# Head of the last product: rebuilding the weight bits with ScalarE's help, and another order of the splits

## The chip, the cores and the metric

The kernel runs on one core of a Trainium2 chip. TensorE (PE in the profile) does the matrix products, VectorE (DVE), ScalarE (ACT) and GpSimd (POOL) prepare operands and drain results, and SyncE (SP) issues the transfers. The metric is device microseconds of one execution; lower is better. Before the change three runs took 577.69, 578.14 and 578.86 us; the median is 578.14 us.

## The reference

Causal attention over 2 batches, 12 heads, 448 positions and 64 dimensions gives `x` of 896 x 768. Two dense blocks follow:

```python
h = x @ w_in                    # 768 -> 2048
g = h * np.cos(h)
y = g @ w_out                   # 2048 -> 768
a = y @ w_a                     # 768 -> 1536
b = y @ w_b
out = (a * b @ w_out2).astype(np.float32)   # 1536 -> 768
```

The weights arrive as 64-bit floats; the kernel gets each as two 32-bit words, low and high.

## The kernel before, in words

All activations are held transposed, features on the 128 partitions, tokens in two halves of 448 columns (b = 0, 1). A product of 32-bit precision is made of three passes on TensorE: each operand is split into a rounded part `hi` and a rest `lo`, and hi·hi, hi·lo and lo·hi are summed in PSUM.

**The weights.** SyncE loads one chunk of 64-bit words into a tile `w_raw` (three buffers, L84), and the chunk is then rebuilt as 32-bit floats in place. `w_scale` (L97, ScalarE) multiplies the high words, read as floats, by 2^-112, which moves the exponent. `w_shift` (L105, VectorE) shifts the low words right by 29, which leaves their top three bits. `w_pack` (L110, VectorE) shifts the scaled high words left by 3 and puts the three bits in; `w_sign` (L118, VectorE) puts the sign in. Then `w_hi` (L143, ScalarE) rounds the chunk and `w_lo` (L154, POOL) subtracts; the end of `w_lo` frees the buffer, and the load of the chunk three places later is issued (L160).

**The last product** is a seven-multiplication scheme over 2 x 2 blocks. A chunk of its weight `w_o2` is a "quad" of four 128 x 128 blocks (512 columns); there are 18, three passes p of six quads q. For a quad the scaled high words go into a PSUM bank named `high` (tag `z`, one buffer, L102), so the next quad's scaling waits until `w_sign` has read it. `w_sums` (L125, VectorE) adds three instructions that form the sums of blocks, in the place of the high words. The other operand is a*b, for six pairs of feature tiles c0 to c5: VectorE multiplies (L674) and forms sums t1, t2, t4 (`sums`, L624); `halves` (L633) splits the seven operands b11, t2, b12, t1, b21, b22, t4 into hi (ScalarE) and lo (VectorE or POOL, as a list names them). c0 to c3 are done well before; c4 and c5 only at the end of the a and b products.

**The order** is the program's own: each engine works through its instructions in the order in which the code issues them, and waits where an operand is missing. `both` (L666) does one pair of a and b products and hangs preparation work `between` and `after` them. `bits_to(i)` rebuilds quads up to i, `halves_of(i)` also splits quad i, and `scale_next` issues the scaling of the next quad not yet rebuilt. In the first pass (L781) step q splits quad q+3, prepares some operands of c5 (`some`), rebuilds quad q+4 and multiplies quad q by seven operands (21 matmuls). Quads 4 and 5 are then multiplied operand by operand, and each finished result is taken out of PSUM by VectorE (`take`, L726).

Of the kernel before, what the change touches and what calls it, by code (L numbers as in the profile page):

```python
# [11 lines left out]
I32 = mybir.dt.int32  # L12
ACTF = mybir.ActivationFunctionType
ALU = mybir.AluOpType
# [2 lines left out]
P = 128  # L17
TWO_PI = 6.283185307179586
SIGN = -0x80000000


def f32(ap):
    return ap.bitcast(F32)
# [3 lines left out]
def tile_causal_attention_cos_gate_bilinear(  # L27
# [16 lines left out]
    nc = tc.nc  # L44
# [5 lines left out]
    N_IN, N_Y, N_C = w_in.shape[0], w_out.shape[0], w_a.shape[0]  # L50
# [15 lines left out]
    QUAD = 4 * P  # L66
# [4 lines left out]
    queue = []  # L71
# [8 lines left out]
    raw, scaled, chunks = {}, {}, {}  # L80
# [13 lines left out]
    def is_quad(i):  # L94
        return queue[i][0] in QUADS

    def w_scale(i):  # L97


        if i < len(queue):  # L100
            high = f32(raw[i][:, :, 1])
            scaled[i] = bank("z", "high")[:, :QUAD] if is_quad(i) else high  # L102
            nc.scalar.activation(scaled[i], high, ACTF.Copy, scale=2.0**-112)  # L103

    def w_shift(i):  # L105
        if i < len(queue):
            low = raw[i][:, :, 0]
            nc.vector.tensor_single_scalar(low, low, 29, op=ALU.logical_shift_right)  # L108

    def w_pack(i):  # L110

        if i < len(queue):
            low, high = raw[i][:, :, 0], scaled[i].bitcast(I32)
            nc.vector.scalar_tensor_tensor(  # L114
                out=low, in0=high, scalar=3, in1=low, op0=ALU.logical_shift_left, op1=ALU.bitwise_or
            )

    def w_sign(i):  # L118
        if i < len(queue):
            low, high = raw[i][:, :, 0], scaled.pop(i).bitcast(I32)  # L120
            nc.vector.scalar_tensor_tensor(  # L121
                out=low, in0=high, scalar=SIGN, in1=low, op0=ALU.bitwise_and, op1=ALU.bitwise_or
            )

    def w_sums(i):  # L125


        if i < len(queue) and is_quad(i):
            t = f32(raw[i]).rearrange("p (s n) w -> p s w n", s=4)
            nc.vector.tensor_tensor(out=t[:, 0, 1], in0=t[:, 0, 0], in1=t[:, 1, 0], op=ALU.subtract)  # L130
            a22 = t[:, 2, 0].unsqueeze(1).to_broadcast([P, 2, P])
            nc.vector.tensor_tensor(out=t[:, 1:3, 1], in0=t[:, 0], in1=a22, op=ALU.add)
            nc.vector.tensor_tensor(out=t[:, 3, 1], in0=t[:, 3, 0], in1=t[:, 2, 1], op=ALU.subtract)
# [40 lines left out]

    def w_bits(i):

        w_shift(i)
        w_pack(i)
        w_sign(i)
        w_sums(i)  # L180

    def w_halves(i):

# [13 lines left out]
    def bank(tag, name):  # L197
        return psum.tile([P, 512], F32, tag=tag, name=name, bufs=BUFS[tag])

    def product(kind, f, acts, name, release, parts=1, pump=True):  # L200

        ps = bank(next(cycle), name)[:, :S]
        n = len(acts)
        t = j = 0
        while t < n:
            hi, lo, k = chunks[kind, f, j]
            terms = [(hi, c, part) for c in range(k) for part in range(2)] + [(lo, c, 0) for c in range(k)]
            for i, (w, c, part) in enumerate(terms):
                nc.tensor.matmul(  # L209
                    ps,  # L210
                    w[:, c * P : (c + 1) * P],
                    acts[t + c][part],
                    start=t == 0 and i == 0,
                    stop=t + k == n and i == len(terms) - 1,
                )
                if (i + 1) % (len(terms) // parts) == 0 and i + 1 < len(terms):
                    yield ps
            t += k
            if release:
                del chunks[kind, f, j]  # L220
            if kind != "in" and pump:
                w_pump()
            j += 1
        yield ps
# [92 lines left out]
    with ExitStack() as actx:  # L317
# [11 lines left out]
        for o in (0, S):  # L329
            for e in range(2):  # L330
                half = mask[e * D : (e + 1) * D, o : o + D]
                nc.gpsimd.affine_select(
                    out=half,
# [174 lines left out]
        def at(fn, i):  # L508
# [25 lines left out]
            (14, w_load, 1),  # L534
            (18, w_load, 2),
            (20, w_scale, 0),
            (22, w_shift, 0),
            (24, w_pack, 0),
# [27 lines left out]
    with tc.manual_schedule():  # L566
# [46 lines left out]
        def plain_tile(q, name):  # L613
            if (q, name) not in plain_tiles:
                pool, tag = plain[q][name]
                plain_tiles[q, name] = pool.tile([P, S], F32, tag=tag, name=f"c{q}_{name}")
            return plain_tiles[q, name]
# [30 lines left out]
        o2_first = len(queue) - (N_Y // 2) * N_Q  # L648
        bits = [o2_first]

        def scale_next():
            if bits[0] not in scaled:
                w_scale(bits[0])

        def bits_to(i):
            while bits[0] <= i:
                scale_next()
                w_bits(bits[0])
                bits[0] += 1

        def halves_of(i):
            bits_to(i)
            scale_next()
            w_halves(i)

        def both(f, b, between=None, after=None, pump=True):  # L666

            q, k = divmod(f, 2)
            ps_b = next(product("b", f, y[b], "b", b == B - 1, pump=pump))
            bs = work.tile([P, S], F32, tag="r", name="bs", bufs=3)  # L670
            nc.scalar.activation(bs, ps_b, ACTF.Copy)  # L671
            between()
            ps_a = next(product("a", f, y[b], "a", b == B - 1, pump=pump))
            nc.vector.tensor_tensor(out=plain_tile(q, f"b{k + 1}{b + 1}"), in0=ps_a, in1=bs, op=ALU.mult)  # L674
            after()

        def items(n):
            def go():
                for _ in range(n):
                    next(todo, None)  # L680
            return go
# [7 lines left out]
        def mixed(*steps):  # L689
            def go():  # L690
                for fn, i in steps:
                    if fn:
                        fn(o2_first + i)
                    else:
                        items(i)()
            return go
# [2 lines left out]
        both(N_C - 2, 0, lambda: None, mixed((bits_to, 0)), False)  # L699
        both(N_C - 1, 0, mixed((bits_to, 1)), lambda: None, False)  # L700
        todo = itertools.chain(sums(IN_G), halves(IN_G, RAWS))
        both(N_C - 2, 1, mixed((None, 4), (halves_of, 0), (None, 1)), mixed((halves_of, 1), (None, 3)), False)
        free[IN_G + 1].insert(0, spare.pop())
        last_sums = sums(IN_G + 1)
        next(last_sums)
        both(N_C - 1, 1, mixed((halves_of, 2), (None, 3)), lambda: None, False)
        assert next(todo, None) is None
        free[IN_G + 1] += free[IN_G]

# [38 lines left out]
                add(kept["v"], ps, kept["v"])  # L748
                store(p, 1, 0, kept["v"])

        BY_DVE = ("b11", "t2", "t1", "b22")
        for _ in last_sums:
            pass
        late = halves(IN_G + 1, BY_DVE)

        DOUBLE = N_Q - 2

        def some(k):
            for _ in range(k):
                next(late)  # L760

        def multiply(p, q, names):
            hi, lo, _ = chunks["o2", p, q]
            for name in names:
                if q == 0:
                    banks[name] = bank(next(cycle), f"o_{name}")[:, :S]
                x_hi, x_lo = cq[q][name, "hi"], cq[q][name, "lo"]
                w = slice(OPS[name] * P, (OPS[name] + 1) * P)
                for i, (w_part, x_part) in enumerate(((hi, x_hi), (hi, x_lo), (lo, x_hi))):
                    nc.tensor.matmul(  # L770
                        banks[name],
                        w_part[:, w],
                        x_part,
                        start=q == 0 and i == 0,
                        stop=q == N_Q - 1 and i == 2,
                    )

        for p in range(N_Y // 2):
            banks, kept = {}, {}
            i = o2_first + p * N_Q  # L780
            for q in range(DOUBLE):  # L781
                halves_of(i + q + 3)
                if p == 0:
                    some((0, 4, 3, 0)[q])
                if (p, q) not in ((0, 3), (1, 0), (1, 1)):
                    bits_to(i + q + 4)
                multiply(p, q, OPS)
                del chunks["o2", p, q]
            for step, name in enumerate(OPS):
                for q in range(DOUBLE, N_Q):  # L790
                    multiply(p, q, [name])
                take(p, name, banks[name], kept)
                if step == (5 if p == 0 else 0):
                    halves_of(i + DOUBLE + 3)
                if step == 6 and p:
                    bits_to(i + N_Q + 2)
            for q in range(DOUBLE, N_Q):
                del chunks["o2", p, q]
            halves_of(i + N_Q + 2)
            if p:  # L800
                bits_to(i + N_Q + 3)
# [56 lines left out]
```

## Time and profile before

| What | Value |
|---|---|
| Runs, median (lowest to highest) | 578.14 us (577.69 to 578.86) |
| The profiled execution | 578.23 us, of which the span of instructions is 576.4 us |
| TensorE busy | 565.1 us, 98% of the span |
| VectorE / ScalarE / POOL busy | 400.0 / 286.2 / 267.4 us |
| Mean granted clock of TensorE | 0.993 of full speed |

The profiled execution is 0.09 us above the median of the runs and holds 1.83 us outside its span. Matmuls overlap, so TensorE's progress is read from the starts of its matmuls: about 0.20 us apart at full clock for 448 columns. A bracket at the end of a row names the idle time of the engine just before it and what ended it.

### The profile page before, as it was taken

Reading aid. Unit: us, or ns where it says so; the run is one execution under the profiler, and the core shown is the slowest. Engines: PE = TensorE matmul, PEld = TensorE weight load, DVE = VectorE, ACT = ScalarE, POOL = GpSimd, SP = SyncE. Lnnn points to the kernel's source line nnn. Section 1 sums busy time; section 2 is a strip of 40 time slices with the busy share of each in tenths; the row PEclk is TensorE's granted clock in tenths of the full one; section 3 lists DMA queues with packets and bytes.
Section 4 is the critical chain, followed back from the end, with each engine's and each line's share of the span. In section 5 each row is a group of like instructions: output and inputs, shape, how many; then the busy total and the mean of one; then the engine's idle time right before and its main releaser. Section 6 shows DMA issues by size and latency. Waiting matters only on the chain.

```text
span 576.4 us, 8792 instructions
## 1 busy us (share of the span) xinstructions
PE 565.1 (98%) x3240; PEld 502.1 (87%) x3240; DVE 400.0 (69%) x704; ACT 286.2 (50%) x582; POOL 267.4 (46%) x242
## 2 busy tenths in 40 slices
PE   8999999999999999999999999999999999989997
PEld 5666789999999999999999999999999998868796
DVE  5899937777777865464455665767676667879994
ACT  6888837777777732232224334343443415334431
POOL 4557744666666642232223223434343407454651
PEclk9999999999999999999999999999999999979999
DMA  8745211333332343433243333333333212324441
GB/s 316 265 161 215 89 56 56 109 111 110 110 109 93 109 147 98 140 101 112 82 164 110 114 109 107 109 111 109 111 109 110 73 38 77 97 65 155 145 140 64
DMA packets 16316, 67.81 MB, mean 118 GB/s; under 512 B 1808, under 2 KB 3472, under 8 KB 16272
## 3 DMA queue, kind: packets, MB, share of 16 engines
q1 hardware_dynamic: 16272, 67.25, 35.1%
q8 instruction: 25, 0.41, 0.3%
q14 instruction: 19, 0.16, 0.1%
HBM read 64.49 MB, written 2.75 MB: 117 GB/s over the span
## 4 chain that ended last, share of the span: by engine, by line
PE 82%; DVE 7%; ACT 4%; issue 3%; POOL 2%; DMA 2%; DVEq 0%; POOLq 0%; ACTq 0%
PE h L209 20%; PE y L209 20%; PE b L209 15%; PE a L209 14%; PE o_b L770 3%; PE o_t L770 3%; PE xa L484 2%; PE pt L457 2%; PE s L382 2%; DMA w_raw<-in_w_o 2%; ACT p L429 1%; POOL p L444 1%; POOL w_lo L158 1%; DVE p L405 1%; ACT w_hi L151 1%
## 5 line engine op out<-in xcount | busy, mean ns | idle before, releaser
L158 POOL TENSOR_TENSOR w_lo<-w_raw,w_hi 128x768 fp32r<-128x768 f32 (+2 forms) x94 | 149.3, 1596 | 227.4 <-ACT w_hi L151 165.3
L151 ACT ACTIVATE w_hi<-w_raw 128x768 fp32r<-128x768 f32 (+1 forms) x91 | 70.0, 778 | 172.8 <-DVE w_raw L121 119.0
L114 DVE SCALAR_TENSOR_TENSOR w_raw<-w_raw 128x768 int32<-128x768 int32 (+1 forms) x58 | 90.8, 1565 | 30.2 <-ACT w_raw L103 29.0
L121 DVE SCALAR_TENSOR_TENSOR w_raw<-w_raw 128x768 int32<-128x768 int32 (+1 forms) x58 | 56.2, 969 | 0.4
L444 POOL TENSOR_SCALAR p<-p,sums 128x448 f32<-128x448 f32 (+6 forms) x84 | 40.7, 505 | 27.5 <-DVE mn L405 26.2
L103 ACT ACTIVATE w_raw<-w_raw 128x768 f32<-128x768 f32 (+1 forms) x58 | 50.8, 876 | 0.0
L108 DVE TENSOR_SCALAR w_raw<-w_raw 128x768 int32<-128x768 int32 (+1 forms) x76 | 50.1, 659 | 0.4 <-DMA w_raw<-in_w_o 0.4
L429 ACT ACTIVATE p<-p,mn 128x448 f32<-128x448 f32 (+6 forms) x84 | 41.8, 501 | 8.4 <-DVE mn L405 8.4
L249 DVE SCALAR_TENSOR_TENSOR r<-r,h 128x448 f32<-128x448 int32 x32 | 19.7, 616 | 25.8 <-ACT r L248 25.7
L405 DVE CUSTOM_DVE_ANT_0 p<-s,mask 128x448 f32<-128x448 f32 (+6 forms) x84 | 31.9, 414 | 4.4 <-PE s L382 4.3
L103 ACT ACTIVATE high<-w_raw 128x512 f32<-128x512 f32 x18 | 11.6, 644 | 41.8 <-DVE w_raw L121 30.9
L382 PE MATMUL s<-qk_raw 64*64 64x448 f32 (+6 forms) x336 | 27.3, 399 | 0.8 <-DMA qk_raw<-in_qk 0.7
L674 DVE TENSOR_TENSOR c_b<-a,bs 128x448 f32<-128x448 f32 x24 | 14.9, 622 | 17.8 <-PE a L209 17.8
L382 PEld LDWEIGHTS s<-qk_raw 64*64 64x64 f32 x336 | 15.5, 135 | 11.5 <-issue 4.0
L248 ACT ACTIVATE r<-h 128x448 int32<-128x448 f32 x32 | 17.1, 539 | 16.0 <-PE h L209 8.3
L457 PE MATMUL pt<-ident,p 128*128 128x128 f32 x168 | 23.9, 280 | 1.0 <-POOL p L444 0.6
L484 PEld LDWEIGHTS xa<-pp,v 128*64 128x64 f32 x336 | 16.1, 137 | 9.4 <-issue 7.1
L484 PE MATMUL xa<-pp,v 128*64 128x64 f32 (+3 forms) x336 | 23.8, 293 | 0.0
L457 PEld LDWEIGHTS pt<-ident,p 128*128 128x128 f32 x168 | 18.2, 140 | 3.7 <-POOL p L444 2.0
L671 ACT ACTIVATE bs<-b 128x448 f32<-128x448 f32 x24 | 12.9, 536 | 15.9 <-PE b L209 15.9
L265 DVE SCALAR_TENSOR_TENSOR r<-r,h 128x448 f32<-128x448 f32 x32 | 19.5, 609 | 1.3 <-ACT r L260 1.3
L470 DVE COPY pp<-pt 128x512 f32<-128x512 f32 (+1 forms) x24 | 14.8, 615 | 6.4 <-PE pt L457 6.3
(357 smaller groups left out, 1671.8 us busy)
## 6 DMA issues: line engine op xcount, KB each, us to landing
w_raw<-in_w_in SPq DMA_DIRECT2D x16, 768.0 KB, 4.4
w_raw<-in_w_out SPq DMA_DIRECT2D x12, 768.0 KB, 4.4
w_raw<-in_w_b SPq DMA_DIRECT2D x12, 768.0 KB, 4.3
w_raw<-in_w_a SPq DMA_DIRECT2D x12, 768.0 KB, 4.4
w_raw<-in_w_o SPq DMA_DIRECT2D x18, 512.0 KB, 3.8
v<-in_v SPq DMA_DIRECT2D x12, 448.0 KB, 5.9
qk_raw<-in_qk SPq DMA_DIRECT2D x11, 448.0 KB, 6.5
w_raw<-in_w_out SPq DMA_DIRECT2D x6, 512.0 KB, 3.9
```

The lines of the kernel that those rows point to most:

```text
L103: nc.scalar.activation(scaled[i], high, ACTF.Copy, scale=2.0**-112)
L108: nc.vector.tensor_single_scalar(low, low, 29, op=ALU.logical_shift_right)
L114: nc.vector.scalar_tensor_tensor(out=low, in0=high, scalar=3, in1=low, op0=ALU.logical_shift_left, op1=ALU.bitwise_or)
L121: nc.vector.scalar_tensor_tensor(out=low, in0=high, scalar=SIGN, in1=low, op0=ALU.bitwise_and, op1=ALU.bitwise_or)
L151: nc.scalar.activation(pair[0][:, a:z], src, ACTF.Copy)
L158: engine.tensor_tensor(out=lo[:, a:z], in0=src, in1=f32(hi)[:, a:z], op=ALU.subtract)
L209: nc.tensor.matmul(ps, w[:, c * P : (c + 1) * P], acts[t + c][part], start=t == 0 and i == 0, stop=t + k == n and i == len(terms) - 1,)
L382: nc.tensor.matmul(T["s", i + c][q, o : o + WIDTH[j]], t[h, Q_COL[j] : Q_COL[j] + D], t[h, FIRST[j] : FIRST[j] + WIDTH[j]], start=True, st ...
L429: nc.scalar.activation(t, t, ACTF.Exp, bias=T["mn", n][:, c], scale=-1.0, accum_out=row_sum(n, j))
L444: nc.gpsimd.tensor_scalar(out=t, in0=t, scalar1=row_sum(n, j), scalar2=1.0, op0=ALU.mult, op1=ALU.mult)
L457: nc.tensor.transpose(dst, p_bufs[n % N_P][:, o : o + P], ident)
L484: nc.tensor.matmul(ps[e * D : (e + 1) * D, o * D : w * D], t[:, k, e], p[:, :, :, q].rearrange("p s l q -> p (s l) q") if k < 3 else p[:, ...
```

## The change

It touches only the 18 quads of `w_o2` and the order of the work around the start of the last product.

```diff
+TOP_SCALE = 2.0**-29 * (1 - 2.0**-10)
+TOP_BIAS = 7.5 * 2.0**-10 - 0.5
...
             high = f32(raw[i][:, :, 1])
-            scaled[i] = bank("z", "high")[:, :QUAD] if is_quad(i) else high
-            nc.scalar.activation(scaled[i], high, ACTF.Copy, scale=2.0**-112)
+            nc.scalar.activation(high, high, ACTF.Copy, scale=2.0**-112)
+            scaled[i] = high
+            if is_quad(i):
+                scaled[i] = bank("z", "top")[:, :QUAD].bitcast(I32)
+                low = raw[i][:, :, 0].bitcast(mybir.dt.uint32)
+                nc.scalar.activation(scaled[i], low, ACTF.Copy, bias=TOP_BIAS, scale=TOP_SCALE)
...
     def w_bits(i):
-        w_shift(i)
-        w_pack(i)
-        w_sign(i)
-        w_sums(i)
+        if i < len(queue):
+            low, high, top = raw[i][:, :, 0], raw[i][:, :, 1], scaled.pop(i)
+            for out_, by, op in ((top, SIGN, ALU.bitwise_and), (low, 3, ALU.logical_shift_left)):
+                nc.vector.scalar_tensor_tensor(out=out_, in0=high, scalar=by, in1=top, op0=op, op1=ALU.bitwise_or)
+            w_sums(i)
...
         def scale_next():
-            if bits[0] not in scaled:
+            if bits[0] in raw and bits[0] not in scaled:
                 w_scale(bits[0])
...
-        both(N_C - 2, 1, mixed((None, 4), (halves_of, 0), (None, 1)), mixed((halves_of, 1), (None, 3)), False)
+        items(4)()
+        bits_to(o2_first + 2)
+        items(2)()
+        both(N_C - 2, 1, mixed((None, 1), (halves_of, 0), (None, 4)), mixed((w_halves, 1)), False)
...
-        both(N_C - 1, 1, mixed((halves_of, 2), (None, 3)), lambda: None, False)
+        both(N_C - 1, 1, mixed((w_halves, 2), (bits_to, 3)), lambda: None, False)
...
-        BY_DVE = ("b11", "t2", "t1", "b22")
+        BY_DVE = ("b12", "b21", "b22")
...
                 halves_of(i + q + 3)
-                if p == 0:
-                    some((0, 4, 3, 0)[q])
                 if (p, q) not in ((0, 3), (1, 0), (1, 1)):
                     bits_to(i + q + 4)
+                if p == 0:
+                    some((5, 2, 0, 0)[q])
                 multiply(p, q, OPS)
```

ScalarE now scales the high words in place in SBUF and, in a second instruction, turns the low words (as unsigned integers) into their top three bits, in the PSUM bank. VectorE puts the sign into that bank and then makes the packed word, two instructions in place of three. Quad 2 and quad 3 are rebuilt earlier, and for c5 another set of lo parts is VectorE's: three (b12, b21, b22) where it had four, so POOL has four (b11, t2, t1, t4) where it had three.

VectorE between the sums of c4 and the last a*b multiplication, before (`w_raw_4346` is quad 2, `w_raw_4484` quad 3):

```order
L630 TENSOR_TENSOR c4_t4_4474<-c4_b21_4271,c4_t2_4472 128x448
L640 TENSOR_TENSOR c4_b11lo_4487<-c4_b11_4150,c4_b11hi_4486 128x448
L674 TENSOR_TENSOR c5_b12_4509<-a_4490,bs_4467 128x448
L640 TENSOR_TENSOR c4_b12lo_4524<-c4_b12_4207,c4_b12hi_4523 128x448
L630 TENSOR_TENSOR c5_t1_4531<-c5_b12_4509,c5_b11_4390 128x448
L108 TENSOR_SCALAR w_raw_4346<-w_raw_4346 128x512
L114 SCALAR_TENSOR_TENSOR w_raw_4346<-high_4476,w_raw_4346 128x512
L121 SCALAR_TENSOR_TENSOR w_raw_4346<-high_4476,w_raw_4346 128x512
```

and in the changed program (`w_raw_4502` is quad 3):

```order
L638 TENSOR_TENSOR c4_t4_4453<-c4_b21_4271,c4_t2_4451 128x448
L187 SCALAR_TENSOR_TENSOR top_4456<-w_raw_4346,top_4456 128x512
L187 SCALAR_TENSOR_TENSOR w_raw_4346<-w_raw_4346,top_4456 128x512
L137 TENSOR_TENSOR w_raw_4346<-w_raw_4346 128x128
L139 TENSOR_TENSOR w_raw_4346<-w_raw_4346 128x256
L140 TENSOR_TENSOR w_raw_4346<-w_raw_4346 128x128
L648 TENSOR_TENSOR c4_b11lo_4464<-c4_b11_4150,c4_b11hi_4463 128x448
L648 TENSOR_TENSOR c4_b12lo_4493<-c4_b12_4207,c4_b12hi_4492 128x448
```

Quad 2 has moved ahead of the first lo part of c4, and its shift is gone.

ScalarE from the last `bs` copy on, before (`w_raw_4517` is quad 4):

```order
L671 ACTIVATE bs_4552<-b_4533 128x448
L103 ACTIVATE high_4560<-w_raw_4484 128x512
L151 ACTIVATE w_hi_4562<-w_raw_4346 128x384
L151 ACTIVATE w_hi_4562<-w_raw_4346 128x512
L638 ACTIVATE c4_b21hi_4570<-c4_b21_4271 128x448
L638 ACTIVATE c4_b22hi_4574<-c4_b22_4335 128x448
L638 ACTIVATE c4_t4hi_4578<-c4_t4_4474 128x448
L103 ACTIVATE high_4614<-w_raw_4517 128x512
L151 ACTIVATE w_hi_4616<-w_raw_4484 128x384
```

and in the changed program (`w_raw_4547` is quad 4):

```order
L679 ACTIVATE bs_4570<-b_4551 128x448
L158 ACTIVATE w_hi_4572<-w_raw_4346 128x384
L158 ACTIVATE w_hi_4572<-w_raw_4346 128x512
L105 ACTIVATE w_raw_4502<-w_raw_4502 128x512
L110 ACTIVATE top_4581<-w_raw_4502 128x512
L105 ACTIVATE w_raw_4547<-w_raw_4547 128x512
L110 ACTIVATE top_4615<-w_raw_4547 128x512
L158 ACTIVATE w_hi_4617<-w_raw_4502 128x384
L158 ACTIVATE w_hi_4617<-w_raw_4502 128x512
```

The split of quad 3 still stands behind the scaling of quad 4, which now is two instructions; the splits of c4 have moved ahead of the `bs` copy.

POOL from the lo part of the last a-and-b chunk on, before (`w_lo_4479`, `w_lo_4512` and `w_lo_4563` are quads 0, 1 and 2):

```order
L158 TENSOR_TENSOR w_lo_4479<-w_raw_4241,w_hi_4478 128x384
L158 TENSOR_TENSOR w_lo_4479<-w_raw_4241,w_hi_4478 128x512
L158 TENSOR_TENSOR w_lo_4512<-w_raw_4305,w_hi_4511 128x384
L158 TENSOR_TENSOR w_lo_4512<-w_raw_4305,w_hi_4511 128x512
L640 TENSOR_TENSOR c4_t2lo_4520<-c4_t2_4472,c4_t2hi_4519 128x448
L640 TENSOR_TENSOR c4_t1lo_4528<-c4_t1_4469,c4_t1hi_4527 128x448
```

and in the changed program (`w_lo_4497` and `w_lo_4542` are quads 0 and 1):

```order
L648 TENSOR_TENSOR c4_t2lo_4468<-c4_t2_4451,c4_t2hi_4467 128x448
L165 TENSOR_TENSOR w_lo_4497<-w_raw_4241,w_hi_4496 128x384
L165 TENSOR_TENSOR w_lo_4497<-w_raw_4241,w_hi_4496 128x512
L648 TENSOR_TENSOR c4_t1lo_4505<-c4_t1_4448,c4_t1hi_4504 128x448
L648 TENSOR_TENSOR c4_t4lo_4517<-c4_t4_4453,c4_t4hi_4516 128x448
L165 TENSOR_TENSOR w_lo_4542<-w_raw_4305,w_hi_4541 128x384
```

Three lo parts of c4 now stand ahead of the lo part of quad 1. On TensorE and SyncE the order is the same as before.

## Rows read from the trace of the kernel before

**Rows 1.** The page, part 1: TensorE; busy us (share of the span) and instructions.

```profile
PE 565.1 (98%) x3240; PEld 502.1 (87%) x3240; DVE 400.0 (69%) x704; ACT 286.2 (50%) x582; POOL 267.4 (46%) x242
```

**Rows 2.** Windows: stretch, length, busy PE, PEld, DVE, ACT, POOL, PEclk, DMA.

```profile
490.40:504.80 14.40, 14.40 (x69) 12.86 (x69) 12.68 (x20) 5.44 (x10) 6.50 (x6) 1.00 0.31 101
504.80:507.40 2.60, 0.11 (x2) 0.01 (x1) 2.39 (x5) 1.14 (x3) 0.00 (x0) 0.93 0.04 14
507.40:513.60 6.20, 6.16 (x16) 5.00 (x17) 4.39 (x6) 2.63 (x6) 5.06 (x4) 0.50 0.27 85
...
539.80:573.00 33.20, 33.05 (x163) 30.17 (x162) 26.55 (x47) 10.90 (x19) 15.01 (x13) 1.00 0.33 107
```

**Rows 3.** Timeline of TensorE: start, length, instruction, [idle before and releaser].

```profile
490.39 0.47 PE L770 MATMUL o_t<-c_t4hi,w_hi 128*128 128x448 f32 x1 [0.85 <-DVE c_b L674]
...
507.39 0.74 PE L770 MATMUL o_b<-c_b11hi,w_hi 128*128 128x448 f32 x1 [2.49 <-ACT w_hi L151]
...
510.96 0.57 PE L770 MATMUL o_t<-c_t2hi,w_lo 128*128 128x448 f32 x1
...
513.57 0.50 PE L770 MATMUL o_t<-c_t1hi,w_hi 128*128 128x448 f32 x1
...
538.40 0.47 PE L770 MATMUL o_b<-c_b11hi,w_hi 128*128 128x448 f32 x1 [0.82 <-ACT w_hi L151]
```

**Rows 4.** Chain of waits in order of time: start, length, engine and instruction.

```profile
498.68 1.16 DVE w_raw L133
...
501.02 1.37 DVE c_b11lo L640
...
506.24 0.63 ACT high L103
...
510.16 1.37 DVE w_raw L108
...
518.94 0.35 DVE w_raw L108
...
524.46 5.17 DMA w_raw<-in_w_o
...
529.72 0.66 ACT high L103
```

**Rows 5.** Timeline of VectorE, the first lo part of c4.

```profile
477.57 0.63 DVE L640 TENSOR_TENSOR c_b11lo<-c_b,c_b11hi 128x448 fp32r<-128x448 f32 x1 [3.10 <-ACT c_b11hi L638]
```

**Rows 6.** Groups by form, from 450 us (ScalarE 440): count, busy us, mean ns.

```profile
L114 DVE SCALAR_TENSOR_TENSOR w_raw<-high,w_raw 128x512 int32<-128x512 int32 x18 | 12.5, 693 | 2.3 <-ACT high L103 1.0
L108 DVE TENSOR_SCALAR w_raw<-w_raw 128x512 int32<-128x512 int32 x18 | 10.0, 557 | 0.4 <-DMA w_raw<-in_w_o 0.4
L114 DVE SCALAR_TENSOR_TENSOR w_raw<-w_raw 128x768 int32<-128x768 int32 x2 | 1.9, 958 | 0.1
L103 ACT ACTIVATE high<-w_raw 128x512 f32<-128x512 f32 x18 | 11.6, 644 | 41.8 <-DVE w_raw L121 30.9 <-DMA w_raw<-in_w_o 7.2 <-DVE w_raw L130 3.7
L151 ACT ACTIVATE w_hi<-w_raw 128x384 fp32r<-128x384 f32 x18 | 9.8, 543 | 1.2 <-DVE w_raw L121 1.2
L103 ACT ACTIVATE w_raw<-w_raw 128x768 f32<-128x768 f32 x2 | 1.8, 890 | 0.0
L158 POOL TENSOR_TENSOR w_lo<-w_raw,w_hi 128x512 fp32r<-128x512 f32 x18 | 24.8, 1378 | 4.2 <-ACT w_hi L151 4.2
L158 POOL TENSOR_TENSOR w_lo<-w_raw,w_hi 128x384 fp32r<-128x384 f32 x18 | 18.9, 1048 | 47.9 <-ACT w_hi L151 42.4 <-PE o_t L770 4.9 <-DVE w_raw L132 0.6
L640 POOL TENSOR_TENSOR c_t4lo<-c_t,c_t4hi 128x448 fp32r<-128x448 f32 x3 | 4.4, 1480 | 1.9 <-ACT c_t4hi L638 1.2 <-DVE c_b21lo L640 0.6
```

**Rows 7.** Timeline of POOL.

```profile
476.65 5.38 POOL L158 TENSOR_TENSOR w_lo<-w_raw,w_hi 128x384 fp32r<-128x384 f32 x4 [14.71 <-ACT w_hi L151]
...
500.60 1.31 POOL L158 TENSOR_TENSOR w_lo<-w_raw,w_hi 128x512 fp32r<-128x512 f32 x1 [0.93 <-ACT w_hi L151]
```

**Rows 8.** Transfers: issue, count, KB each, median us from issue to landing.

```profile
w_raw<-in_w_o SPq DMA_DIRECT2D x17, 512.0 KB, 3.8
```

## The prediction

> **What bounds the kernel now.** The page's first part comes first: TensorE is busy for 98% of the span [rows 1], so time can only come from the few places where it stands or runs slowly. The windows of the last product show them [rows 2]: from 504.8 to 507.4 us TensorE does almost nothing, and from 507.4 to 513.6 us its granted clock is 0.50, which is the lower level of 1.2 GHz. From 539.8 us on it has no gap, and 163 matmuls in 33.20 us give the pace of an unhindered one, 0.204 us.
>
> The timeline of TensorE names what it waited for [rows 3]: at 490.39 us for a VectorE multiplication (call it stall A, 0.85 us); at 507.39 us for the hi part of quad 5, for 2.49 us (stall B, with the slow stretch behind it); at 538.40 us for a hi part of the second pass (stall C, 0.82 us, and some shorter waits round it, about 2 us in all). B is the large one. The chain of waits tells why that hi part is late [rows 4]: ScalarE scales for quad 6 at 506.24 us just before it, because VectorE has only then released the PSUM bank; and before that VectorE's own queue is the chain, through the sums of quad 4 (1.16 us at 498.68) and the lo parts of c5 (1.37 us at 501.02). In the window before the stall VectorE is busy for 12.68 of 14.40 us, POOL for 6.50 and ScalarE for 5.44 [rows 2]. So at the head VectorE sets the end, while earlier it had stood idle for 3.10 us before 477.57 [rows 5].
>
> **The change part by part.** *VectorE.* For each quad the shift goes, 0.557 us on average over 18 [rows 6], of which the ones beside POOL took far longer (1.37 us at 510.16 [rows 4]). The two instructions that stay read one SBUF and one PSUM operand as before, but the first now writes PSUM, which no row of VectorE here shows. Bounds: the shift's 0.557 us below, 0.958 us above, the mean of the same form on 768 elements; I take 0.693 us, the row of the same form and width. Quad 2 moves into the 3.10 us of idle time. Between that point and quad 5's last packing instruction VectorE thus loses quad 2's place (0.557 + 2 x 0.693 plus three sums, about 3 us), three shifts (1.7 us) and one lo part. It was needed at 506.24; now it is ready near 500. VectorE is no longer what quad 5 waits for.
>
> *ScalarE.* It gains one instruction for each quad, reading SBUF and writing PSUM over 128 x 512. The nearest row is the scaling itself, 0.644 us; bounds 0.543 us (the 384-wide split) and 0.890 us (768 wide) [rows 6]. The scaling now goes to SBUF and no longer waits for the bank; only the new instruction does. So where the bank decides, the chain has one instruction after the wait, as before, and costs nothing more. Where the landing of a load decides, there are two in a row, 0.64 us more, with the hi part of the quad before queued behind them on ScalarE.
>
> *POOL, which is late next.* Three lo parts of c4 now stand ahead of quad 1's. Before, quad 1's lo part ended at 476.65 + 5.38 = 482.03 us [rows 7]; with three times 1.48 us [rows 6] ahead of it, it ends at 486.5. Its end issues the load of quad 4, which lands 3.8 us later [rows 8], at 490.3. ScalarE waits for that landing, and behind it in its queue stands the hi part of quad 3: 490.3 + 0.64 + 0.64 + 0.54 and some hundredths for handing over is 492.2 us. From there POOL has, up to the end of quad 5, three quads of 1.048 + 1.378 = 2.43 us and the four lo parts of c5 of 1.48 us: 13.2 us, so 505.4. Quad 5's second part also needs its hi part, behind VectorE's sums; a wait of that kind is 0.93 us at 500.60 [rows 7]. I add it: 506.3 us. Without it 505.4; with the one slow load, 5.17 us at 524.46 [rows 4], in place of 3.8 it is 507.7.
>
> *What it comes to.* Leave stall A as it is (the last multiplication now stands behind quad 3's rebuilding instead of two lo parts, about as much). The first matmul that needs quad 5's second lo part is the 78th from 490.39 on, so an unhindered TensorE reaches it at 490.39 + 77 x 0.204 = 506.1. POOL lets it go at 506.35. Before, that matmul started at 510.96 [rows 3]: 4.6 us gained. Behind it seven matmuls ran slowly to 513.57, 2.61 us where 7 x 0.204 = 1.43 would do: 1.2 us more. In the second pass two scalings that a landing releases (529.72 is one [rows 4]) get a second instruction behind them, at most 1.3 us; against it one shift leaves the chain (0.35 us at 518.94) and another stands no longer ahead of the first pass's results (1.37 us at 510.16) [rows 4]. Net between 0.4 gained and 1.3 lost; I take 0.2 lost, nearer the gain, since the results of the first pass no longer queue behind late rebuilding. Sum: 4.6 + 1.2 - 0.2 = 5.6 us. The profiled execution took 578.23 us, 0.09 above the median, which is less than the runs differ: 572.6 us.
>
> The uncertain prices: with the new ScalarE instruction at 0.890 and both VectorE instructions at 0.958 each quad's chain grows by 0.25 + 0.53 = 0.78 us, and some four such links stand between the head and the end of the second pass, so up to 3.1 us, 575.7. Below, with quicker instructions, TensorE itself is the limit.
>
> **The rivals.** *The clock falls in the head after all* (B). The row shows 1.2 GHz after one idle stretch of 2.49 us [rows 3] and 0.50 over 6.2 us behind it [rows 2]. If the shorter waits that I leave do the same, 15 matmuls take 6.2 us in place of 3.1: 3.1 us of the gain stay away, 575.7 us. Against it: after the waits at 538.40 the window shows 1.00 [rows 2]. The Trainium skill's page "TensorE: Matmul & The Clock Gate", section "A second HAM failure mode: psum-queue depth-cycling", tells of a kernel in which short, frequent idle moments between groups of matmuls were enough to make the clock fall again. The traces here so far speak for the single long idle stretch, so this rival has the smaller chance.
>
> *Everything is hidden* (C). POOL's last wait does not arise, stall A goes (the multiplication is no longer late) and the second pass loses half its 2 us: 5.6 + 2 = 7.6 us, 570.6. For it: VectorE is eased everywhere. Against it: POOL holds 13.2 us of work for 13.9 us of time.
>
> *The lead is given back* (D). If the ring of three buffers, not the first pass, sets when the second pass's quads come, stall C grows by what the head gained, and the time stays at about 578. For it: loads of 5.17 and 3.8 us lie on the chain there [rows 4]. Against it: they are issued by POOL's lo parts, which follow VectorE's work on the first pass's results, and those follow TensorE.
>
> *POOL becomes a worse bound than VectorE was* (E, slower). Its price is set at one place, the end of quad 5's lo part. With a load of 5.17 us and each of its ten instructions held up by a VectorE subtraction for about 0.3 us the end comes at 506.3 + 1.4 + 3.0 = 510.7. TensorE then stands for over 4 us, and the clock falls as it did: 572.6 + 4.4 + 3.1 = 580.1. It decides from the point at which the end lies later than 506.3 + 5.6 - 3.1, about 508.8. For it: four lo parts in a row on POOL. Against it: the four instructions of quads 0 and 1 took 5.38 us with VectorE beside them [rows 7], 0.13 us each over the means.
>
> **How the numbers follow.** The forecast has 0.62, with its own range 571.2 to 574.3 (the bounds of POOL's end and of the second pass). B 0.15, C 0.10, D 0.07, E 0.06. The range reaches from C's 570.6 to 575.9, past B and the uncertain prices; outside lie D, E and the outer half of C. A change under 0.2%, 1.2 us, could not be told from none. Faster: the forecast, B, C and a little of D, 0.88. Same: 0.06. Slower: 0.06.
>
> **What would show it.** Right: no wait of TensorE over 1.5 us in the head; granted clock 1.00 through the first pass; the matmul of t2 with quad 5's lo part near 506.4 us; VectorE's first new instruction near 0.69 us and ScalarE's near 0.64; a wait of ScalarE's scaling for the load of quad 4 near 490; POOL busy without a break from 492 to 506. Wrong: a stretch at 0.50 (B), TensorE waiting for POOL past 508.8 (E), a stall C of 4 us or more (D), or new instructions of 0.9 us.

## The result and the profile after

Four runs of the changed kernel took 573.31, 571.19, 570.83 and 570.50 us, median 571.01; beside them the kernel before took 577.99. The ratio is 0.9885, interval 0.9856 to 0.9914: 7.0 us less, where 5.6 were forecast. A second measurement, told below, gave 570.72 us and 0.9875 (0.9861 to 0.9889). The profiled execution is the slowest of the four, 573.31 us with a span of 571.5.

The only wait of a matmul in the head, and those of the second pass (timeline of the changed kernel; the lines of the code moved, L781 is the matmul):

```profile
505.54 0.47 PE L781 MATMUL o_t<-c_t2hi,w_lo 128*128 128x448 f32 x1 [0.23 <-POOL w_lo L165]
...
526.43 0.47 PE L781 MATMUL o_t<-c_t2hi,w_lo 128*128 128x448 f32 x1 [0.38 <-POOL w_lo L165]
532.00 0.47 PE L781 MATMUL o_b<-c_b11hi,w_hi 128*128 128x448 f32 x1 [1.38 <-ACT w_hi L158]
533.10 0.47 PE L781 MATMUL o_b<-c_b11hi,w_lo 128*128 128x448 f32 x1 [0.43 <-POOL w_lo L165]
```

Against [rows 3]: stalls A and B are gone, the matmul of t2 with quad 5's lo part starts at 505.54 instead of 510.96, and stall C comes at 532.00 instead of 538.40, but is 1.38 us long where it was 0.82. The windows (length, busy PE, PEld, DVE, ACT, POOL, granted clock, DMA):

```profile
489.60:505.00 15.40, 15.40 (x77) 14.21 (x77) 14.81 (x18) 10.79 (x20) 12.15 (x10) 1.00 0.31 100
505.60:517.00 11.40, 11.40 (x57) 10.58 (x58) 9.41 (x19) 5.95 (x11) 4.64 (x4) 1.00 0.45 152
...
534.00:537.00 3.00, 3.00 (x10) 2.59 (x10) 2.64 (x6) 2.67 (x5) 1.40 (x3) 0.53 0.49 142
```

Through the first pass the clock is 1.00, where [rows 2] show 0.50 for 6.20 us. In this run it is 0.53 behind stall C; ten matmuls in 3.00 us, where 0.204 apart they would take 2.0.

POOL and ScalarE at the head (timelines), then the new instructions (groups by form from 450 us, ScalarE's from 440; count, busy us, mean ns):

```profile
483.23 5.00 POOL L165 TENSOR_TENSOR w_lo<-w_raw,w_hi 128x384 fp32r<-128x384 f32 x4
491.54 2.32 POOL L165 TENSOR_TENSOR w_lo<-w_raw,w_hi 128x384 fp32r<-128x384 f32 x2 [3.31 <-ACT w_hi L158]
...
504.17 1.32 POOL L165 TENSOR_TENSOR w_lo<-w_raw,w_hi 128x512 fp32r<-128x512 f32 x1 [0.99 <-ACT w_hi L158]
```

```profile
489.79 0.67 ACT L105 ACTIVATE w_raw<-w_raw 128x512 f32<-128x512 f32 x1 [4.95 <-DMA w_raw<-in_w_o]
```

```profile
L187 DVE SCALAR_TENSOR_TENSOR top<-w_raw,top 128x512 int32<-128x512 int32 x18 | 12.4, 690 | 7.1 <-ACT top L110 7.1
L187 DVE SCALAR_TENSOR_TENSOR w_raw<-w_raw,top 128x512 int32<-128x512 int32 x18 | 12.4, 690 | 1.9
L110 ACT ACTIVATE top<-w_raw 128x512 int32<-128x512 uint32 x18 | 11.3, 626 | 8.7 <-DVE w_raw L187 8.6
```

ScalarE waits at 489.79 for the load of quad 4, POOL starts behind it at 491.54 and works up to quad 5's lo part with two breaks, of 0.32 us at 501.98 and of 0.99 us. Each new instruction costs about what its nearest row said.

The chain of waits shows what sets the time behind the first pass (start, length, engine):

```profile
510.90 0.62 DVE ou L731
...
512.23 0.70 DVE w_raw L187
...
514.14 2.34 POOL w_lo L165 x2
...
516.50 5.76 DMA w_raw<-in_w_o
...
522.91 0.61 ACT top L110
523.53 0.48 ACT w_hi L158
...
526.40 3.81 DMA w_raw<-in_w_o
...
531.42 0.53 ACT w_hi L158
...
533.10 0.47 PE o_b L781
```

Two transfers lie in it, each issued at the end of a lo part, and behind each landing stand ScalarE's scaling, its new instruction and only then a hi part of the quad before. In [rows 4] the same places read 518.94 for VectorE's quad 7 and 524.46 for the transfer.

### The profile page after: what moved, and what is told of

Same layout as the page of the kernel before. It is cut to its first block, busy times and chain, and to the rows that moved or that the text cites. A ratio compares the mean times of both kernels' runs of the same rounds, so it can differ in the third digit from the quotient of the medians.

```text
span 571.5 us, 8805 instructions
## 1 busy us (share of the span) xinstructions
PE 562.5 (98%) x3240; PEld 501.3 (88%) x3240; DVE 395.8 (69%) x685; ACT 296.3 (52%) x600; POOL 267.9 (47%) x243
## 4 chain that ended last, share of the span: by engine, by line
PE 85%; DVE 6%; ACT 3%; POOL 3%; DMA 2%; issue 2%; POOLq 0%; DVEq 0%; ACTq 0%
PE h L217 21%; PE y L217 20%; PE b L217 15%; PE a L217 15%; PE o_b L781 4%; PE o_t L781 3%; PE xa L492 2%; PE pt L465 2%; PE s L390 2%; DMA w_raw<-in_w_o 2%; ACT p L437 1%; POOL w_lo L165 1%; POOL p L452 1%; DVE p L413 1%; ACT w_hi L158 1%
## 5 line engine op out<-in xcount | busy, mean ns | idle before, releaser
L105 ACT ACTIVATE w_raw<-w_raw 128x768 f32<-128x768 f32 (+1 forms) x76 | 62.7, 826 | 18.8 <-DMA w_raw<-in_w_o 17.4
L115 DVE TENSOR_SCALAR w_raw<-w_raw 128x768 int32<-128x768 int32 (+1 forms) x58 | 40.1, 692 | 0.0
L263 ACT ACTIVATE r<-r 128x448 f32<-128x448 f32 x32 | 18.3, 571 | 0.0
L268 ACT ACTIVATE r<-r 128x448 f32<-128x448 f32 x32 | 18.2, 568 | 0.0
```

What stands on the lines that cost most here:

```text
L105: nc.scalar.activation(high, high, ACTF.Copy, scale=2.0**-112)
```

## Experiments

Each time is a median, with its ratio to the kernel before (run beside it) and the interval; where a time is set against the changed kernel, 570.9 us is meant, the middle of its eight runs in two measurements. The same code stands a few lines higher or lower in each kernel.

**1. The new instructions with the old order.** Only the instructions of the change (two on ScalarE, two on VectorE for a quad); lists of `both`, `some` and `BY_DVE` as before.

> The new instructions (top bits by ScalarE, two instructions on VectorE for each quad) with the order of the kernel before. Theory (the order makes the gain): ScalarE's scaling of the next quad still stands late in its queue and each quad's chain is one ScalarE instruction of about 0.62 us longer, one VectorE shift of 0.56 us shorter, so stall B stays at over 2 us, the clock falls behind it, and the time is 577 to 579 us. Rival (the lighter VectorE makes it): three shifts less between quad 2's place and quad 5, 3 x 0.557 = 1.7 us, come off the 2.49 us of stall B; the rest of it is too short for the clock to fall, so 1.7 + 1.2 us are gained: 575 us, or 573 if the whole stall goes.

577.71 us, 1.0005 (0.9994 to 1.0016): nothing. Stall B is there (TensorE, ScalarE and VectorE, timelines):

```profile
506.79 0.74 PE L777 MATMUL o_b<-c_b11hi,w_hi 128*128 128x448 f32 x1 [2.31 <-ACT w_hi L157]
```

```profile
505.64 0.63 ACT L109 ACTIVATE top<-w_raw 128x512 int32<-128x512 uint32 x1 [2.93 <-DVE w_raw L186]
506.20 1.29 ACT L157 ACTIVATE w_hi<-w_raw 128x384 fp32r<-128x384 f32 x2
```

```profile
500.79 1.37 DVE L647 TENSOR_TENSOR c_b11lo<-c_b,c_b11hi 128x448 fp32r<-128x448 f32 x1 [1.26 <-ACT c_b11hi L645]
```

VectorE still waits, 1.26 us here (1.20 us at 501.02 in the kernel before), for hi parts that ScalarE makes late: c5's stand behind quad 4's, and quad 5's behind the new instruction for quad 6. Of the time of the three shifts, some 1.4 us with the gaps behind them, VectorE keeps about 0.4 up to quad 5; most of the rest goes into a further wait of 0.46 us at 493.50 and into sums of quad 4 that run longer. Stall B ends 0.6 us earlier in this execution (506.79 for 507.39), and the medians show nothing of it. The theory holds.

**2. The new order with the old instructions.** `w_scale`, `w_shift`, `w_pack` and `w_sign` of before in the changed kernel.

> The new order with the old instructions (shift, pack, sign on VectorE; ScalarE scales into the PSUM bank). Theory (the order makes the gain): quad 5 is rebuilt some 6 us before it was needed, so 1.7 us of shifts more on VectorE are still covered; the head has no wait of TensorE over 1 us and the time is 571 to 572 us. Rival (the lighter VectorE is needed): the shifts and the bank that is free only after the third VectorE instruction bring quad 5 late again; a wait of 1.5 us or more near 505 to 507 us with a slow stretch behind it, 574 to 577 us.

573.23 us, 0.9918 (0.9905 to 0.9932): 4.7 of the 7 us. Both theories miss by some: no wait of 1.5 us, but two of nearly half that one after the other, and 1.2 us more than expected.

```profile
504.85 0.47 PE L776 MATMUL o_b<-c_b11hi,w_hi 128*128 128x448 f32 x1 [0.82 <-ACT w_hi L154]
506.23 0.47 PE L776 MATMUL o_b<-c_b11hi,w_lo 128*128 128x448 f32 x1 [0.71 <-POOL w_lo L161]
```

Quad 5 is late by little now, and the old instructions make it late; the run doesn't tell the shift from the bank, which comes free later with them. Taken alone the new instructions were worth nothing, behind the new order they are worth some 2 us.

**3. The lo parts of c5 shared out as before.**

```diff
-        BY_DVE = ("b12", "b21", "b22")
+        BY_DVE = ("b11", "t2", "t1", "b22")
```

> The changed kernel with the lo parts of c5 shared out as before: VectorE has b11, t2, t1, b22, POOL b12, b21, t4. Theory (POOL's work is what is late next in the head): POOL has one lo part of 1.2 to 1.3 us less before quad 5's lo part, so the wait of 0.23 us at 505.54 goes, VectorE has slack for it, and the time stays within 0.5 us of the changed kernel, 570.5 to 571.5. Rival (the sharing-out is what eased VectorE): four lo parts of 0.63 us, the first ones among them, make VectorE late for quads 4 and 5 again; TensorE waits 1 us or more between 500 and 507, and the time is 572.5 or more.

571.06 us, 0.9885 (0.9872 to 0.9899): the same, as the theory has it. Its reason isn't shown, though. The wait of the matmul at 505.54 is gone, but POOL, with one lo part less, waits 1.61 us for quad 5's hi part (at 502.70) and ends at 505.31, only 0.18 us earlier than in the changed kernel; and number 11, with POOL's work unchanged, has no such wait either. Stall C is 1.50 us at 531.76 here. Taking this part of the change back costs nothing.

**4. Quads 2 and 3 in their old place**, all else as changed.

```diff
-        items(4)()
-        bits_to(o2_first + 2)
-        items(2)()
-        both(N_C - 2, 1, mixed((None, 1), (halves_of, 0), (None, 4)), mixed((w_halves, 1)), False)
+        both(N_C - 2, 1, mixed((None, 4), (halves_of, 0), (None, 1)), mixed((halves_of, 1), (None, 3)), False)
...
-        both(N_C - 1, 1, mixed((w_halves, 2), (bits_to, 3)), lambda: None, False)
+        both(N_C - 1, 1, mixed((halves_of, 2), (None, 3)), lambda: None, False)
```

> The changed kernel, but quads 2 and 3 are rebuilt and the first quads split where the kernel before has them (new instructions and new handling of c5 stay). Theory (the gain comes from the place of quads 2 and 3: VectorE works on them in what was 3.10 us of idle time): VectorE idles there again and everything up to quad 5 is some 3 us later; quad 5's rebuilding ends near 503 instead of 500.7, its parts near 506 to 507, TensorE waits 1 to 2 us near 504 and the time is 572.5 to 575. Rival (the handling of c5, three lo parts for VectorE and quads 3 and 4 ahead of them, makes the gain): no more waiting than now, 571.

574.84 us, 0.9953 (0.9937 to 0.9969): 3.9 us of the gain are lost, as the theory has it. The edit also takes back the order in which c4 and the first quads are split, so the 3.9 us belong to both together. VectorE's idle time is back, and so is a wait for quad 5; stall A is back too, with 0.98 us. The profiled execution is the slowest of the seven, 578.01 us, so its waits may be longer than the median's:

```profile
478.21 0.62 DVE L648 TENSOR_TENSOR c_b11lo<-c_b,c_b11hi 128x448 fp32r<-128x448 f32 x1 [3.13 <-ACT c_b11hi L646]
```

```profile
506.21 0.47 PE L778 MATMUL o_b<-c_b11hi,w_hi 128*128 128x448 f32 x1 [1.34 <-ACT w_hi L158]
507.46 0.74 PE L778 MATMUL o_b<-c_b11hi,w_lo 128*128 128x448 f32 x1 [0.57 <-POOL w_lo L165]
```

**5. c5 handled as before**, all else as changed: `some((0, 4, 3, 0)[q])` in its old place ahead of `bits_to`, and the old `BY_DVE`.

> The changed kernel, but c5 is handled as in the kernel before: its seven operands are split behind quads 4 and 5 in fours and threes, and VectorE has the lo parts b11, t2, t1, b22. Theory (the place of quads 2 and 3 makes the gain): VectorE has one lo part more, 0.63 us, ahead of quad 5, which was ready some 4 us before it was needed; 571 to 572 us and no wait over 0.5 us in the head. Rival (the handling of c5 makes it): stall B is back with over 1.5 us, 574 or more.

573.07 us, 0.9916 (0.9904 to 0.9929). The head has no wait, as the theory says, and yet 2 us are lost: neither foresaw where. TensorE waits in the second pass for a result of the first (TensorE, VectorE, ScalarE):

```profile
517.28 0.47 PE L781 MATMUL o_t<-c_t4hi,w_hi 128*128 128x448 f32 x1 [1.41 <-DVE ov L731]
```

```profile
504.39 1.16 DVE L648 TENSOR_TENSOR c_b22lo<-c_b,c_b22hi 128x448 fp32r<-128x448 f32 x1 [1.74 <-ACT c_b22hi L646]
...
510.58 0.62 DVE L731 TENSOR_TENSOR ou<-o_t,oa 128x448 f32<-128x448 f32 x1 [1.23 <-ACT oa L740]
```

```profile
510.03 0.52 ACT L740 ACTIVATE oa<-o_b 128x448 f32<-128x448 f32 x1
```

c5's last splits stand between quads 5 and 6, so quad 6 is rebuilt late, the copy `oa` stands behind its hi part, and VectorE's first result comes at 510.58; in the changed kernel it comes at 507.65. This was the first sign of the term that the forecast lacks.

**6. The hi part of quad 9 ahead of the scaling of quad 10** (ScalarE's queue alone).

```diff
             bits_to(i)
-            scale_next()
-            w_halves(i)
+            if i - o2_first not in (9,):
+                scale_next()
+            w_hi(i)
+            if i - o2_first in (9,):
+                scale_next()
+            w_lo(i, nc.gpsimd)
```

> The changed kernel with one swap on ScalarE: the hi part of quad 9 stands ahead of the scaling of quad 10 instead of behind it. Theory (part of the second pass's waits is ScalarE's queue: hi parts that are ready stand behind a scaling that waits for a transfer): bits of quad 9 were ready at 518.8 and its hi part ran at 523.5; now it runs near 519, quad 9's lo part ends some 4.5 us earlier and the load behind it goes out at about 522 instead of 526.4; the wait of 1.38 us for quad 10 near 532 goes or shrinks below 0.5, and the time is 569.5 to 570.5. Rival (the transfers' own length sets it): the waits stay and the time with them, 571.0; if the scaling of quad 10 then comes late, 572.

569.57 us, 0.9855 (0.984 to 0.9869), as expected. The interval overlaps that of the second measurement of the changed kernel, but the slowest of the four runs, 569.96 us, is under the fastest of that kernel's eight, 570.47. The long wait is gone; one of 0.71 us is left:

```profile
532.38 0.47 PE L785 MATMUL o_t<-c_t2hi,w_lo 128*128 128x448 f32 x1 [0.71 <-POOL w_lo L165]
```

So part of stall C is a hi part that is ready and stands behind an instruction that waits for a transfer.

**7. Quad 7 split at the first step of the first pass's end**, in the changed kernel.

```diff
-                if step == (5 if p == 0 else 0):
+                if step == 0:
```

> The changed kernel with the rebuilding and splitting of quad 7 hung after the first operand of the first pass's end (step 0) in place of the sixth (step 5), so that the loads of quads 8 to 10 are issued earlier. Theory (the second pass's waits come from VectorE's and ScalarE's late start on quads 7 to 9, not from the transfers themselves): the waits between 526 and 534 us, 0.38 + 1.38 + 0.43 in the profiled execution, go, the clock stays at 1.00 and the time is about 571.0 - 2.5 = 568.5 us. Rival (the ring of three buffers and transfers of 3.8 to 5.8 us set it): the waits move to another quad of the second pass and the time stays at 571; or quad 7's work delays the results of the first pass and its end, 572.

569.24 us, 0.9851 (0.9838 to 0.9865). TensorE waits nowhere between 490 and 540 us (windows):

```profile
490.00:507.00 17.00, 17.00 (x84) 15.43 (x83) 16.26 (x22) 12.16 (x23) 13.23 (x11) 1.00 0.29 97
507.00:526.00 19.00, 19.00 (x93) 17.25 (x93) 16.80 (x29) 9.82 (x19) 9.87 (x10) 1.00 0.55 180
526.00:540.00 14.00, 14.00 (x69) 12.71 (x69) 13.25 (x21) 7.85 (x14) 8.07 (x7) 1.00 0.38 116
```

The same transfers, issued earlier, are hidden. This is the lowest median, 1.5 us under the second measurement of the changed kernel (whose interval it just touches; the slowest run here, 569.63 us, is under the fastest there) and 8.6 under the kernel before; from number 6 it can't be told apart.

**8. The same line in the kernel before**, and **9. in the new order with the old instructions.**

> The kernel before with one line of the best version so far: quad 7's rebuilding and splitting after the first operand of the first pass's end instead of the sixth. Theory (stall C is a matter of quad 7's place alone and has nothing to do with the change): the waits between 530 and 540 us, about 2 us in all, go here too, and the time is 576 us. Rival (in the kernel before VectorE is too late for an earlier place: quad 6 is rebuilt only after 508): the work on quad 7 goes in front of the results of the first pass without any gain, 577 to 578.5 us.

> The new order with the old instructions and with quad 7's splitting at step 0. Theory (the waits of the second pass go with the early quad 7 whatever the instructions are): of the waits of the new order with the old instructions those of the second pass, 0.47 + 0.65 + 0.43 us, go, those of the head, 0.82 + 0.71, stay: 573.2 - 1.5 = 571.7 us. Rival (with the shift VectorE is too late for the early place): the results of the first pass wait behind quad 7, 573 or more.

Number 8: 576.43 us, 0.9976 (0.9968 to 0.9985), as the theory has it, though not quite by its way: stall C goes, and TensorE waits 1.97 us for a result of the first pass at 518.59 instead. Number 9: 571.38 us, 0.9875 (0.986 to 0.989), 1.9 less than number 2; its two waits of the head, 0.79 and 0.72 us, are what is left of the long ones. Stall C is a matter of quad 7's place and apart from the change.

**10. ScalarE's new instruction issued twice.**

> The changed kernel with ScalarE's new instruction (the top bits) issued twice for each quad. Theory (about four links of each chain between the head and the end of the second pass hold this instruction, as the forecast's upper bound has it): 4 x 0.62 = 2.5 us more, 573.5, between 572.5 and 575. Rival (ScalarE is busy for half the span, and it is hidden): 571 to 571.5.

574.80 us, 0.9942 (0.993 to 0.9955): 3.9 us over the changed kernel, beyond the 2.5 named and within the range. So the instruction isn't hidden. The count of links isn't borne out: between 478 and 541 us the chain of waits holds the doubled instruction only twice, at 491.72 and 533.19, 1.3 us in all. TensorE's waits grow at more places: they are 0.62 at stall A, 0.51 at 505.43, and 0.45, 0.39, 1.83 and 0.42 in the second pass, where the changed kernel's first profile had 0.23, 0.38, 1.38 and 0.43. How they add up to 3.9 us is not shown.

**11. The changed kernel again**, and **12. the kernel before again**, for second profiles.

> The changed kernel once more, for a second profile and a time beside the runs of this call. In the first profile the granted clock was 0.53 from 534 to 537 us, behind waits of 1.38 and 0.43 us, and nine matmuls there cost 1.5 us too much; that run took 573.31, the three others 570.50 to 571.19. Theory (the slow stretch is an accident of single runs): 570.5 to 571.5 us as median; a profile with the same waits of 1.2 to 1.5 us and a clock of 1.00 behind them takes about 571. Rival (the slow stretch belongs to the kernel): 0.5 again in the profile, and a median of 572 or more.

570.72 us, 0.9875 (0.9861 to 0.9889). TensorE waits 0.74 us at 530.68 and the clock stays at 1.00:

```profile
530.68 0.47 PE L781 MATMUL o_b<-c_b11hi,w_hi 128*128 128x448 f32 x1 [0.74 <-ACT w_hi L158]
531.79 0.47 PE L781 MATMUL o_b<-c_b11hi,w_lo 128*128 128x448 f32 x1 [0.42 <-POOL w_lo L165]
```

```profile
532.00:540.00 8.00, 8.00 (x40) 7.30 (x40) 7.46 (x12) 4.87 (x9) 4.91 (x5) 1.00 0.42 135
```

The slow stretch of the first profile doesn't belong to every run of the kernel. What the clock does behind the same waits this profile can't say, as its wait is half as long; number 3 had the longer waits and 1.00. The first transfer of the chain took 4.82 us here, not 5.76, which is more than the wait is shorter.

> The kernel before once more, for a second profile; its runs show mean clocks of 0.993 to 0.997 without a difference in time. Theory (a slow stretch with a wait behind it costs nothing at the end): with a mean clock near 0.997 the stretch at 0.50 behind stall B is shorter or missing, stall C and the waits round it are longer by 1 us or more, and the time is 577 to 578.5. Rival (the slow matmuls behind stall B cost 1.2 us at the end, as the forecast counted them): stall C as it was, and with a shorter slow stretch a time 0.5 to 1.2 us below 577.9.

578.45 us, a single execution. Stall B is the same 2.49 us, but the clock behind it is 0.72 (0.50 in [rows 2]):

```profile
507.40:513.60 6.20, 6.10 (x21) 5.04 (x22) 4.30 (x6) 2.62 (x6) 5.07 (x4) 0.72 0.27 85
```

```profile
507.46 0.74 PE L770 MATMUL o_b<-c_b11hi,w_hi 128*128 128x448 f32 x1 [2.49 <-ACT w_hi L151]
...
522.52 0.47 PE L770 MATMUL o_t<-c_t4hi,w_hi 128*128 128x448 f32 x1 [1.30 <-DVE ov L720]
```

```profile
515.35 0.62 DVE L720 TENSOR_TENSOR ou<-o_t,oa 128x448 f32<-128x448 f32 x1 [1.18 <-ACT oa L729]
```

TensorE had done its matmuls earlier and then waited 1.30 us for VectorE's result; that wait isn't in the first profile. The second pass's first t4 matmul of its first quad starts at 522.52 here and at 522.43 there. So the theory holds in kind (a slow stretch that has a wait behind it costs nothing at the end), with another wait than the stall C that it named.

## Why the prediction was right, and what its sum lacked

**Mechanism.** Stall B went because quad 5 comes early, as forecast. The earlier place of quads 2 and 3, with the order of the first splits, carries it (number 4: 3.9 us); the new instructions count only behind it (numbers 1 and 2: 0 alone, 2.3 on top); which lo parts of c5 VectorE makes counts for nothing (number 3), and where c5's splits stand counts 2 us (number 5).

**The range.** 7.0 us were gained where the sum has 5.6. The measured 571.01 us lies below the forecast's own range, 571.2 to 574.3, and inside the outer one because that reaches to rival C's 570.6. The inner range also doesn't come out of the bounds that it names: added up, with TensorE itself not there before 506.1, they give 571.8 to 575.1. Of C's three conditions one came true, that stall A goes.

**Step by step.** VectorE's last packing for quad 5 started at 500.07 (forecast near 500). The prices hold: 690 ns against 693, 626 against 644. ScalarE waited for quad 4's load until 489.79 (490.3), POOL started behind it at 491.54 (492.2), had a wait of 0.99 us (0.93) ahead of quad 5's second part, and let TensorE go at 505.54 (506.35). That is 5.4 us earlier than before, where 4.6 were forecast. The way there is another one, though. The forecast takes POOL's 13.2 us of work as the bound and says that "VectorE is no longer what quad 5 waits for". The chain of waits of the changed kernel goes through VectorE, and POOL is only its last link:

```profile
500.07 0.70 DVE w_raw L187
...
500.79 1.04 DVE w_raw L137
...
502.32 1.02 DVE w_raw L140
...
503.42 0.68 ACT w_hi L158
...
504.17 1.33 POOL w_lo L165
...
505.54 0.47 PE o_t L781
```

Quad 5's sums end at 503.34, 2.6 us after its packing. That POOL's end came near the forecast is in part luck: number 3 takes a lo part from POOL, and its end moves by 0.18 us. In the second profile (number 11) TensorE doesn't wait there at all; that matmul starts at 505.40.

Nor did stall A stay "as it is". The last multiplication starts at 488.76 instead of 489.72, and TensorE waits 0.34 us, in the weight load alone (PEld):

```profile
489.43 0.19 PEld L781 LDWEIGHTS o_t<-c_t4hi,w_hi 128*128 128x128 f32 x1 [0.34 <-DVE c_b L682]
```

That is 1.0 us earlier than 490.39. Without it TensorE would have come to the t2 matmul at 506.1, as forecast, and not at 505.1. So 0.6 of the 5.4 us hang on it in the first profile, and all of the 1.0 us in the second, where TensorE waits nowhere from there to 530 us.

**The term that was wrong** is "behind it seven matmuls ran slowly: 1.2 us more". They ran slowly, but their time was not on the path. The second profile of the kernel before shows it: with a clock of 0.72 in place of 0.50 TensorE was earlier, and waited for VectorE's results. Behind stall B it is VectorE that sets the time in the kernel before: quad 6's rebuilding, whose shift alone took 1.37 us at 510.16 [rows 4], then its hi part on ScalarE, the copy `oa` behind that, and the results. VectorE's first result and the last one ahead of quad 7 in the kernel before:

```profile
515.26 0.62 DVE L720 TENSOR_TENSOR ou<-o_t,oa 128x448 f32<-128x448 f32 x1 [1.17 <-ACT oa L729]
...
518.32 0.62 DVE L720 TENSOR_TENSOR ou<-o_b,ou 128x448 f32<-128x448 f32 x1
```

In the changed kernel the first comes at 507.65 (507.29 in the second profile) and no longer sets the time; the last, which quad 7 and the chain follow, comes at 510.90 (510.76), when TensorE has finished its matmuls. That is 7.4 us earlier (7.6). From the t2 matmul to this result it is 5.4 us in both profiles, where it was 7.4 before: 2.0 us gained, in place of the 1.2. Number 5 shows the same link from the other side: with the head free of waits, a first result that comes 3 us later costs 2 us.

**The second pass.** The forecast took 0.2 lost. In the first profile stall C starts 6.40 us earlier than before, so 1.0 of the 7.4 are given back; in the second 7.72, 0.2 more than the head gained. Both lie between the bounds. From the landing of each of the two transfers to the hi part behind it the chain takes about 0.6 us longer than before, 1.1 to 1.2 us for both: that is ScalarE's second instruction, priced at 1.3 at most. Against it some 0.8 us are saved on VectorE and POOL. What parts the two profiles is the transfers, 9.6 us for both in the first and 8.4 in the second (8.9 before). The clock behind stall C then took 1.5 us more in the first profile and nothing in the second: 6.4 - 1.5 = 4.9 us, which is what the profiled execution gained (578.23 to 573.31), and 7.7, which is what the second did. Rival D, the lead given back, is there in small: up to 1.0 us of it.

**The clock rival** did not come true in the head. The case cited with it, on the Trainium skill's page "TensorE: Matmul & The Clock Gate", section "A second HAM failure mode: psum-queue depth-cycling", in which short idle moments are enough, is borne out in part: 0.53 behind waits of 1.38 and 0.43 us in one run of the changed kernel. Number 3 had 1.50 and 0.42 us at the same place and stayed at 1.00. What tells these runs apart isn't settled.

## What to carry to other kernels

Before you move work off an engine, look where it stands idle: moving the rebuilding of quads 2 and 3 forward, the first of them into 3.1 us of idle time, gave 3.9 us together with the new order of the first splits, and taking one of three instructions for each quad off the busy engine gave nothing until that was done. Work out a gain at the engine that sets the end of the stage, not at the stalled one: here a slow stretch of TensorE with a wait behind it was no loss, and its end no gain. Where an engine takes its instructions in order, a ready one behind one that waits for a transfer is a stall of its own; swapping the two, or issuing the transfer earlier, was worth 1.3 and 1.5 us here (numbers 6 and 7).

## What the runs showed of the hardware

The same stall of 2.49 us at the same place was followed by a granted clock of 0.50 over 6.20 us [rows 2], of 0.72 (number 12), and of 1.00 in number 8:

```profile
507.10:513.60 6.50, 6.02 (x28) 5.15 (x29) 4.72 (x7) 2.89 (x6) 5.09 (x4) 1.00 0.27 81
513.60:518.50 4.90, 3.02 (x15) 2.45 (x14) 4.66 (x8) 2.88 (x6) 3.43 (x3) 1.00 0.24 59
518.50:526.00 7.50, 7.10 (x26) 5.91 (x27) 6.95 (x15) 1.99 (x4) 2.12 (x2) 0.77 0.67 221
```

There it fell only behind a second wait, the 1.97 us at 518.59. Two waits of the head, 0.82 and 0.71 us, left it at 1.00 in number 2, and two of 0.79 and 0.72 us were followed by 0.76 from 507.0 to 513.6 us in number 9. How long a wait is did not tell, in these runs, whether the clock falls behind it.
